# Three halves of expert weights moved from the attention part to behind its last cast and later, and the expert part cut finer

## The chip, the cores and the metric

One core of one Trainium2 chip. The metric is the device time of one execution in microseconds (us), lower is better. Unless said otherwise a time is the median of several unprofiled runs, and positions in time ("at 109 us") count from the start of a profiled run's span. A core's five engines work side by side: TensorE (PE, with its weight loads as PEld), VectorE (DVE), ScalarE (ACT), GpSimd (Pool) and SyncE (SP). Sixteen DMA engines move data; in this kernel SP issues the loads of q, k, v and the attention's stores (queue q1 of the profile), Pool issues expert weights, gathers and scatters (queue q0).

## The reference, cut to what matters

```python
# attention: 4 batches x 8 heads, 768 tokens of 64; 3 heads causal, 5 with a window of 64 and 4 sinks
x = attention(q, k, v)                      # [3072, 512]
do_compute = x @ w_skip > 0                 # tokens that go through an expert
e_idx = argmax(x[do_compute] @ w_gate, 1)   # one of 8 experts each
for e in range(8):
    h = relu(xc[e_idx == e] @ w1[e])        # 512 -> 1024
    y[e_idx == e] = gate * (h @ w2[e])      # 1024 -> 512
out = x;  out[do_compute] += y
```

The weights are 8 x 2 matrices of 512 x 1024 in float32: 33.6 MB to read. "A half" below is one of these 16 matrices (1 MB once cast to 16 bits), "a quarter" half of it.

## The kernel before

Attention runs over 16 pairs of heads. Results go to `out` in DRAM; then each expert's rows are gathered from `out`, worked on, and scattered back. Weights are loaded in a fixed order from a list, wherever the program calls for the next ones, so all of them share one queue in the order of the calls.

```python
todo = [(e, half, qt) for e in range(E) for half in range(2) for qt in range(2)]

def load_weight(quarters=2):
    e, half, q0 = todo[0]
    del todo[:quarters]
    nc.gpsimd.dma_start(out=<tile of e, half>, in_=<weights, float32>)   # cut

# weigh(i, hi): values of pair i (cut)
    if not last:
        ins = nc.gpsimd.tensor_copy(x16s[i], xh[:, :, h2:h2 + 2])
        if i in (0, 5, 10, 11, 12, 13):
            with tc.issue_after(ins.ins):
                load_weight()

# gate_transpose(i) (cut)
    if i == NPR - 2:
        nc.gpsimd.drain()
    if i == NPR - 1:
        nc.gpsimd.tensor_copy(mark, xTg[:, 0, :1])
        load_weight()

# expert part
    gather(0, 4); load_weight(1)
    gather(4, 6); load_weight(1)
    gather(6, 8); load_weight()
    rows(0); first(0); rows(1)
    for e in range(E):
        if e + 2 < E:
            first(e + 1)
            t = 4 * (e + 2)
            if t < NT:
                gather(t, t + 4)
            if todo:
                load_weight(1 if len(todo) == 2 else 2)
            rows(e + 2)
        second(e)            # its two scatters are issued here, by Pool
        # ... (cut)
```

`load_weight` takes two quarters unless told otherwise. `rows` casts and transposes an expert's 256 gathered rows, `first` and `second` are its two products. `nc.gpsimd.drain()` is an instruction at which Pool's queue stands still for a while; how long, and behind what, the traces below show. The values of `v` arrive in two buffers, so pair i + 2 is loaded once pair i is cast by Pool (`cast_v`).

The softmax here doesn't subtract the row's maximum and nothing guards it: scores larger than these inputs give would overflow.

Of the kernel before, what the change touches and what calls it, by code (L numbers as in the profile page):

```python
# [9 lines left out]
FP32 = mybir.dt.float32  # L10
FP16 = mybir.dt.float16
# [4 lines left out]
ACT = mybir.ActivationFunctionType  # L16
# [11 lines left out]
DM = H * D  # L28
E = 8
# [4 lines left out]
P = 128  # L34

DS = DM // P
FS = F // P
CAP = 256
# [3 lines left out]
WR = 4  # L42
# [217 lines left out]
def kernel(  # L260
# [14 lines left out]
    nc = tc.nc  # L275
    C = Consts()
# [77 lines left out]
    wts = {}  # L354
# [19 lines left out]
    def load_weight(quarters=2):  # L374

        e, half, q0 = todo[0]
        q1 = q0 + quarters
        assert q1 <= 2
        del todo[:quarters]
        if half == 0:  # L380
            w = DS * F // 2
            nc.gpsimd.dma_start(
                out=wts[e, 0].rearrange("p s f -> p (s f)")[
                    :, q0 * w:q1 * w], in_=w1r[e][:, q0 * w:q1 * w])
        else:
            nc.gpsimd.dma_start(
                out=wts[e, 1].rearrange("p (t r) d -> p t (r d)", r=WR)[
                    :, q0:q1],
                in_=w2r[e][:, q0:q1])
# [20 lines left out]
    with tc.tile_pool(name="ac", bufs=1) as ac_pool, \  # L410
# [29 lines left out]
        NPR = B * H // 2  # L440
# [62 lines left out]
        def cast_v(i):  # L503
            va, vx = vab[i % 2], vxb[i % 2]
            nc.gpsimd.tensor_copy(va[:, :, :, :D], v32[i])  # L505
            if i:
                nc.scalar.activation(xgs[i], xgs[0], ACT.Copy)  # L507
            for hi, hh in enumerate(heads(i)[1]):
                if not IS_RETR[hh]:
                    nc.gpsimd.tensor_copy(vx[:, hi], va[:, hi, :NQB - 1])  # L510
                    nc.gpsimd.tensor_copy(
                        vx[:N_SINK, hi], va[:N_SINK, hi, 0:1].to_broadcast(
                            [N_SINK, NQB - 1, D + 1]))

        def transpose(i, name):
            tps = tr_psum.tile([P, S], FP16, tag="tps", name="tps")
# [92 lines left out]
        def weigh(i, hi):  # L609
            b, hs = heads(i)  # L610
            b0 = base(i, hi)
            va, vx = vab[i % 2], vxb[i % 2]
            if IS_RETR[hs[hi]]:
                plan = [(qb, RCOL[j, qb], va[:, hi, j])
                        for qb in range(NQB) for j in range(qb + 1)]
            else:
                plan = []
                for qb in range(NQB):
                    plan.append((qb, qb * P, va[:, hi, qb]))
                    if qb:  # L620
                        plan.append((qb, (NQB - 1 + qb) * P,
                                     vx[:, hi, qb - 1]))
            opsa = ov_psum.tile([P, NQB, D + 1], FP32, tag="opsa",
                                name="opsa")
            for n, (qb, c, vb) in enumerate(plan):
                nc.tensor.matmul(  # L626
                    opsa[:, qb, :], ats[i][:, b0 + c:b0 + c + P], vb,
                    start=(n == 0), stop=(n == len(plan) - 1))
            if i % 2 == 0 and hi == 0:
                xhs[i // 2] = x_pool.tile([P, NQB, 4, D], FP32, tag="xh",  # L630
                                          name="xh")
            last = i == NPR - 1
            if hi == 0:
                x16s[i] = gat_pool.tile([P, NQB, 2, D], FP16, tag="gx16",
                                        name="gx16", bufs=2)
            rec = o_pool.tile([P, NQB, 1], FP32, tag="rec", name="rec")
            nc.vector.reciprocal(rec, opsa[:, :, D:D + 1])  # L637
            if last:
                nc.vector.tensor_mul(x16s[i][:, :, hi], opsa[:, :, :D],
                                     rec.to_broadcast([P, NQB, D]))  # L640
            nc.vector.tensor_mul(xhs[i // 2][:, :, 2 * (i % 2) + hi, :],  # L641
                                 opsa[:, :, :D],
                                 rec.to_broadcast([P, NQB, D]))
            if hi == 0:
                return
            xh = xhs[i // 2]
            h2 = 2 * (i % 2)
            if not last:
                ins = nc.gpsimd.tensor_copy(x16s[i], xh[:, :, h2:h2 + 2])  # L649
                if i in (0, 5, 10, 11, 12, 13):  # L650
                    with tc.issue_after(ins.ins):
                        load_weight()
            if i >= NPR - 2:
                nc.sync.dma_start(
                    out=Ov[b][:, :, hs[0] * D:(hs[1] + 1) * D].rearrange(
                        "p n (h d) -> p n h d", h=2),
                    in_=xh[:, :, h2:h2 + 2])
            elif i % 2 == 1:
                hc = (i // 2) % 2
                nc.sync.dma_start(  # L660
                    out=Ov[b][:, :, hc * 4 * D:(hc + 1) * 4 * D],
                    in_=xh.rearrange("p n h d -> p n (h d)"))
# [250 lines left out]
    with tc.tile_pool(name="moe_w", bufs=1) as mw_pool, \  # L913
# [19 lines left out]
        def gather(t0, t1):  # L933
            for t in range(t0, t1):
                ins = nc.gpsimd.indirect_dma_start(  # L935
                    out=xgs[t], out_offset=None, in_=out[:, :],
                    in_offset=bass.IndirectOffsetOnAxis(
                        ap=idx_s[:, t:t + 1], axis=0),
                    bounds_check=N - 1, oob_is_err=False)
                apart(ins)  # L940
                gathers[t] = ins.ins

        xTs, hts = {}, {}

        def rows(e):

            xT = mx_pool.tile([P, DS, CAP], FP16, tag="xT", name="xT")
            x16s = []
            for s2 in range(NSM):
                x16 = mx_pool.tile([P, DM], FP16, tag="x16", name="x16")  # L950
                nc.vector.tensor_copy(
                    x16.rearrange("p (s r) -> p s r", s=DS),
                    xgs[e * NSM + s2].rearrange("p (r s) -> p s r", s=DS))
                x16s.append(x16)
            for s2, x16 in enumerate(x16s):
                xtp = xt_psum.tile([P, DS, P], FP16, tag="xtp", name="xtp")
                for s in range(DS):
                    nc.tensor.matmul(xtp[:, s, :], x16[:, s * P:(s + 1) * P],
                                     C.ident, is_transpose=True,
                                     start=True, stop=True)  # L960
                nc.vector.tensor_copy(xT[:, :, s2 * P:(s2 + 1) * P], xtp)  # L961
            xTs[e] = xT

        def first(e):
            ht = h_pool.tile([P, FS, CAP], FP16, tag="ht", name="ht")
            for f2 in range(FS // 2):
                hps = h_psum.tile([P, 2, CAP], FP32, tag="hps", name="hps")
                for fi in range(2):
                    fs = 2 * f2 + fi
                    for s in range(DS):  # L970
                        nc.tensor.matmul(  # L971
                            hps[:, fi, :],
                            wts[e, 0][:, s].rearrange(
                                "p (t c r) -> p t r c", c=P, r=WR)[
                                    :, fs // WR, fs % WR],
                            xTs[e][:, s, :], start=(s == 0),
                            stop=(s == DS - 1))
                nc.scalar.activation(ht[:, 2 * f2:2 * f2 + 2], hps, ACT.Relu)  # L978
            hts[e] = ht
# [33 lines left out]
        with tc.manual_schedule(engines={mybir.EngineType.Pool,  # L1013
                                         mybir.EngineType.PE,
                                         mybir.EngineType.DVE}):
            gather(0, 4)
            load_weight(1)
            gather(4, 6)
            load_weight(1)
            gather(6, 8)  # L1020
            load_weight()
            rows(0)
            first(0)
            rows(1)
            for e in range(E):
                if e + 2 < E:
                    first(e + 1)
                    t = 4 * (e + 2)
                    if t < NT:
                        gather(t, t + 4)  # L1030
                    if todo:
                        load_weight(1 if len(todo) == 2 else 2)
                    rows(e + 2)
                second(e)
                if e == E - 2:
                    first(e + 1)
                if todo:
                    load_weight(1 if len(todo) < 3 else 2)
                if e == E - 2:


                    nc.gpsimd.drain()
# [39 lines left out]
```

## Time and profile before

| | before |
|---|---|
| time, median of 4 runs (range) | 206.7 us (205.48 to 207.62) |
| the profiled run | 203.35 us, span 201.9 us |
| DMA, share of 16 engines' span | q0 50.3%, q1 44.3% |
| PE busy / DVE / ACT / POOL | 81% / 54% / 56% / 59% |
| attention's last rows ready, first gather, first product | 120.4, 127.1, 133.1 us |
| last weight lands, PE ends, span ends | 190.4, 192.8, 201.9 us |

How to read it: no compute engine is near full over the whole span, but DMA is, at 94.6%. In the expert part PE has hardly a gap either (59.0 us busy of the 60 from 133 us on). The profiled run is faster than each of the four timed ones, so its 201.9 us of span lies at the fast end. Below, three groups of lines from the kernel before stand for what later changes. First, three stretches of the expert part (stretch, length, then busy us of PE, PEld, DVE, ACT and POOL with numbers of instructions, then PE's granted clock, DMA share, GB/s):

```profile
133.00:146.00 13.00, 12.18 (x103) 10.14 (x103) 5.30 (x11) 4.78 (x8) 10.47 (x11) 1.00 1.00 228
146.00:154.00 8.00, 8.00 (x64) 6.10 (x62) 4.04 (x8) 2.55 (x5) 5.29 (x6) 1.00 1.05 232
154.00:190.40 36.40, 36.40 (x268) 26.38 (x267) 14.53 (x26) 11.79 (x20) 17.70 (x20) 1.00 1.01 236
```

DMA is at 1.00 or a little above in all three (a share above 1 is packets that overlap on an engine). PE is busy for 12.18 of 13 us in the first and to the hundredth in the other two. Second, Pool's drain and the load behind the last transpose (start, length, engine, what):

```profile
L682 POOLq DRAIN  x1: 5147/5147/5147, 115.3 to 115.3; - x1
120.54 0.19 POOL L685 COPY mark<-gxT 128x1 f16<-128x1 f16 x1 [4.27 <-DVE gxT L678]
121.01 0.56 POOL L382 DMA_DIRECT2D w<-in_moe_w_dram  x1 [0.28 <-issue]
127.13 1.10 POOL L935 DMA_INDIRECT xg<-out_dram,idx_s  x1 [4.06 <-DVE flagi L910]
```

The drain took 5.1 us here. It ended at 120.4, 0.5 us after the copy (DVE, at 119.9) that Pool had to wait for next. The routing's next small Pool instruction waited for DVE until 122.6 in any case, so the drain held no gather. Third, the expert 6 products on PE:

```profile
174.88 3.66 PE L971 MATMUL hps<-xT,w 128*128 128x256 f16 x32
```

There is no bracket behind it: PE did not wait for the weights.

### The profile page before, as it was taken

How to read it: one execution, taken by the hardware profiler on the slowest of the kernel's cores; microseconds unless marked ns; L12 is line 12 of the kernel's file. 1: busy time of each engine (PE TensorE's matmuls, PEld its weight loads, DVE VectorE, ACT ScalarE, POOL GpSimd, SP SyncE). 2: the span in 40 equal slices, each digit the busy share in tenths (PEclk: the TensorE clock that was granted, in tenths of full speed). 3: DMA queues.
4: the chain of work that ended last, by engine and by line, in shares of the span. 5: the costliest groups of instructions: out<-in, count | busy, mean ns of one | idle time of the engine just before them, and what ended most of it. 6: DMA issues, size and time to landing. Idle time of an engine off the chain costs nothing.

```text
span 201.9 us, 4741 instructions
## 1 busy us (share of the span) xinstructions
PE 163.2 (81%) x1896; PEld 119.3 (59%) x1896; DVE 109.5 (54%) x254; ACT 113.0 (56%) x164; POOL 119.3 (59%) x179
## 2 busy tenths in 40 slices
PE   0487999889888898888982757978999999999920
PEld 0366666676666676666852443378678678665700
DVE  5323666636899668997650678253444534534020
ACT  5998888897688977888891420035143144130400
POOL 7585499687387693788403901687858575133311
PEclk9999999999999999999998795999999999999985
DMA  5999699999899999999999899479999999999501
GB/s 173 295 345 287 169 174 238 316 327 318 236 245 201 301 343 296 342 266 214 215 275 232 204 234 174 103 181 246 232 239 233 239 245 233 235 245 248 165 14 63
DMA packets 47856, 47.12 MB, mean 233 GB/s; under 512 B 28484, under 2 KB 43588, under 8 KB 46802
## 3 DMA queue, kind: packets, MB, share of 16 engines
q0 software_dynamic: 6976, 21.56, 50.3%
q1 hardware_dynamic: 40850, 25.17, 44.3%
q8 instruction: 17, 0.28, 0.6%
q14 instruction: 13, 0.11, 0.2%
HBM read 56.64 MB, written 10.49 MB: 333 GB/s over the span
## 4 chain that ended last, share of the span: by engine, by line
ACT 27%; DMA 26%; PE 23%; issue 8%; DVE 7%; POOL 6%; POOLq 1%; SPq 0%; ACTq 0%; DVEq 0%
ACT at L606 15%; DMA out_dram<-xg,idx_s 14%; DMA vf<-in_v_dram 10%; PE pst L578 5%; ACT xg L507 4%; PE pst L588 4%; PE hps L971 4%; ACT qT L526 4%; ACT gxT L675 3%; PE opsa L626 3%; POOL out_dram L1001 2%; PE pst L595 2%; PE yps L991 2%; POOL xg L935 2%; DMA xg<-out_dram,idx_s 1%
## 5 line engine op out<-in xcount | busy, mean ns | idle before, releaser
L606 ACT ACTIVATE at<-pst 128x1024 f16<-128x1024 f32 (+2 forms) x76 | 61.3, 836 | 17.2 <-PE pst L600 13.3
L978 ACT ACTIVATE ht<-hps 128x512 f16<-128x512 f32 x32 | 19.1, 598 | 49.4 <-PE hps L971 49.4
L588 PE MATMUL pst<-qT,kz 128*128 128x128 f16 (+2 forms) x288 | 35.8, 242 | 2.5 <-ACT qT L526 2.1
L588 PEld LDWEIGHTS <-kz 128*128 128x128 f16 x288 | 24.1, 100 | 21.9 <-issue 12.8
L535 DVE COPY kz<-tps 64x768 f16<-64x768 f16 x28 | 26.6, 950 | 9.7 <-PE tps L518 9.3
L971 PE MATMUL hps<-xT,w 128*128 128x256 f16 x256 | 29.2, 273 | 1.2 <-DVE xT L961 1.2
L971 PEld LDWEIGHTS <-w 128*128 128x128 f16 x256 | 27.9, 113 | 2.8 <-issue 1.5
L578 PE MATMUL pst<-smask,ident 128*128 128x512 f16 (+1 forms) x60 | 22.3, 372 | 8.7 <-ACT at L606 8.7
L991 PE MATMUL yps<-w,ht 128*128 128x512 f16 x128 | 28.8, 379 | 0.0
L1001 POOL DMA_INDIRECT out_dram<-xg,idx_s x16 | 16.4, 1022 | 18.5 <-issue 8.5
L649 POOL CAST gx<-xh 128x768 f16<-128x768 f32 x15 | 12.4, 828 | 19.3 <-DVE xh L641 14.5
L999 DVE SCALAR_TENSOR_TENSOR xg<-yps,gsl,xg 128x512 f32<-128x512 f32 x16 | 12.0, 750 | 20.4 <-PE yps L991 20.3
L626 PE MATMUL opsa<-va,at 128*128 128x65 f16 x372 | 19.8, 196 | 4.0 <-POOL va L505 4.0
L935 POOL DMA_INDIRECT xg<-out_dram,idx_s x16 | 16.8, 1047 | 8.6 <-issue 4.3
L626 PEld LDWEIGHTS <-at 128*128 128x128 f16 x472 | 17.9, 99 | 5.4 <-issue 4.2
L505 POOL CAST va<-vf 128x768 f16<-128x768 f32 x16 | 14.0, 876 | 11.2 <-DMA vf<-in_v_dram 11.1
L637 DVE RECIPROCAL rec<-opsa 128x6 f32<-128x6 f32 x32 | 6.2, 194 | 26.3 <-PE opsa L626 25.9
L991 PEld LDWEIGHTS <-ht 128*128 128x128 f16 x128 | 12.3, 98 | 13.5
L641 DVE TENSOR_TENSOR xh<-opsa,rec 128x384 f32<-128x384 f32 x32 | 17.8, 556 | 1.3
L499 POOL CAST qin<-qf 128x768 f16<-128x768 f32 x16 | 13.1, 818 | 3.3 <-DMA qf<-in_q_dram 3.3
L499 POOL CAST kin<-kf 128x768 f16<-128x768 f32 x16 | 13.1, 822 | 1.0 <-DMA kf<-in_k_dram 0.8
L518 PE MATMUL tps<-ident,qin 128*128 128x128 f16 x96 | 8.7, 231 | 5.9 <-POOL qin L499 5.9
(117 smaller groups left out, 260.7 us busy)
## 6 DMA issues: line engine op xcount, KB each, us to landing
w<-in_moe_w_dram POOLq DMA_DIRECT2D x14, 1024.0 KB, 10.7
qf<-in_q_dram SPq DMA_DIRECT2D x16, 384.0 KB, 6.3
kf<-in_k_dram SPq DMA_DIRECT2D x16, 384.0 KB, 6.0
vf<-in_v_dram SPq DMA_DIRECT2D x32, 192.0 KB, 6.0
out_dram<-xh SPq DMA_DIRECT2D x7, 768.0 KB, 6.8
w<-in_moe_w_dram POOLq DMA_DIRECT2D x4, 512.0 KB, 12.4
out_dram<-xh SPq DMA_DIRECT2D x2, 384.0 KB, 5.2
xg<-out_dram,idx_s POOLq DMA_INDIRECT x16, 7.2
```

The source lines that it names most:

```text
L499: nc.gpsimd.tensor_copy(h16, qk32[name, i].rearrange("p h n d -> p n h d"))
L535: nc.vector.tensor_copy(to, ti[r])
L578: nc.tensor.matmul(pst[:, bank - c0:bank - c0 + mw], C.ident, rmask.unsqueeze(1).to_broadcast([P, mw // P, P]) if retr else smask[:, bank: ...
L588: nc.tensor.matmul(pst[:, cols], kz[:, j * P:(j + 1) * P], qT[i][:, qb * P:(qb + n) * P], start=mw <= 0, stop=mw <= 0 or last)
L606: nc.scalar.activation(ats[i][:, b0:b0 + cn], pst[:, :cn], ACT.Exp, scale=SCALE)
L626: nc.tensor.matmul(opsa[:, qb, :], ats[i][:, b0 + c:b0 + c + P], vb, start=(n == 0), stop=(n == len(plan) - 1))
L641: nc.vector.tensor_mul(xhs[i // 2][:, :, 2 * (i % 2) + hi, :], opsa[:, :, :D], rec.to_broadcast([P, NQB, D]))
L935: ins = nc.gpsimd.indirect_dma_start(out=xgs[t], out_offset=None, in_=out[:, :], in_offset=bass.IndirectOffsetOnAxis(ap=idx_s[:, t:t + 1], ...
L971: nc.tensor.matmul(hps[:, fi, :], wts[e, 0][:, s].rearrange("p (t c r) -> p t r c", c=P, r=WR)[:, fs // WR, fs % WR], xTs[e][:, s, :], sta ...
L978: nc.scalar.activation(ht[:, 2 * f2:2 * f2 + 2], hps, ACT.Relu)
L991: nc.tensor.matmul(ypss[s2], hts[e][:, fs, s2 * P:(s2 + 1) * P], wts[e, 1][:, fs, :], start=(fs == 0), stop=(fs == FS - 1))
L1001: ins = nc.gpsimd.indirect_dma_start(out=out[:, :], out_offset=bass.IndirectOffsetOnAxis(ap=idx_s[:, t:t + 1], axis=0), in_=xgs[t], in_off ...
```

## The change

Its intent, as one reads it from the code: three halves of weights no longer compete with the last loads of v (Pool waited 10.1 us for one of them), and fill instead the hollow in DMA traffic around the first gathers. The expert part is cut finer so that it can start after one gather.

```diff
 # cast_v(i)
+            if i == NPR - 1:
+                load_weight()
+                load_weight()
 # weigh
-                if i in (0, 5, 10, 11, 12, 13):
+                if i in (0, 5, 10):
 # expert part
-            gather(0, 4)
+            gather(0, 2)
+            load_weight(1)
+            gather(2, 4)
             load_weight(1)
             gather(4, 6)
             load_weight(1)
             gather(6, 8)
-            load_weight()
-            rows(0)
-            first(0)
+            load_weight(2 if len(todo) % 2 == 0 else 1)
+            first_by_tile(0)          # 128 rows at a time: 64 matmuls of 128 columns for 32 of 256
             rows(1)
+            second(0)
+            rows(2)
+            first(1)
             for e in range(E):
+                if 0 < e < E - 2:
+                    first(e + 1)
                 if e + 2 < E:
-                    first(e + 1)
                     t = 4 * (e + 2)
                     if t < NT:
                         gather(t, t + 4)
                     if todo:
-                        load_weight(1 if len(todo) == 2 else 2)
+                        load_weight(1 if len(todo) < 3 or len(todo) % 2 else 2)
-                    rows(e + 2)
-                second(e)
+                    if e:
+                        rows(e + 2)
+                if e:
+                    second(e)
 # (cut: row() and first_by_tile() themselves; the last load's parity)
```

More of the change, by code (lines that the diff above doesn't have):

```diff
@@ L943, with row @@
         xTs, hts = {}, {}
+        def row(e, s2):
+            if s2 == 0:
+                xTs[e] = mx_pool.tile([P, DS, CAP], FP16, tag="xT", name="xT")
+            x16 = mx_pool.tile([P, DM], FP16, tag="x16", name="x16")
+            nc.vector.tensor_copy(
+                x16.rearrange("p (s r) -> p s r", s=DS),
+                xgs[e * NSM + s2].rearrange("p (r s) -> p s r", s=DS))
+            xtp = xt_psum.tile([P, DS, P], FP16, tag="xtp", name="xtp")
+            for s in range(DS):
+                nc.tensor.matmul(xtp[:, s, :], x16[:, s * P:(s + 1) * P],
+                                 C.ident, is_transpose=True,
+                                 start=True, stop=True)
+            nc.vector.tensor_copy(xTs[e][:, :, s2 * P:(s2 + 1) * P], xtp)
         def rows(e):
@@ L962, in rows, with first_by_tile @@
             xTs[e] = xT
+        def first_by_tile(e):
+            ht = h_pool.tile([P, FS, CAP], FP16, tag="ht", name="ht")
+            hpss = [h_psum.tile([P, 2, CAP], FP32, tag="hps", name="hps")
+                    for _ in range(FS // 2)]
+            for s2 in range(NSM):
+                cols = slice(s2 * P, (s2 + 1) * P)
+                if s2 == 0:
+                    row(e, 0)
+                for fs in range(FS):
+                    if s2 == 0 and fs == FS - 3:
+                        row(e, 1)
+                    for s in range(DS):
+                        nc.tensor.matmul(
+                            hpss[fs // 2][:, fs % 2, cols],
+                            wts[e, 0][:, s].rearrange(
+                                "p (t c r) -> p t r c", c=P, r=WR)[
+                                    :, fs // WR, fs % WR],
+                            xTs[e][:, s, cols],
+                            start=(s == 0), stop=(s == DS - 1))
+                    if s2 == NSM - 1 and fs % 2:
+                        nc.scalar.activation(ht[:, fs - 1:fs + 1],
+                                             hpss[fs // 2], ACT.Relu)
+            hts[e] = ht
         def first(e):
@@ L1037 @@
                 if todo:
-                    load_weight(1 if len(todo) < 3 else 2)
+                    load_weight(1 if len(todo) < 3 or len(todo) % 2 else 2)
                 if e == E - 2:
```

## The prediction

> **What bounds the kernel now.** I read the page's slices first, then the chain that ended last, the waits, the Pool timeline around the largest wait, the DMA queues in short windows, and PE and DMA stretch by stretch. The slices show the DMA row at 9 nearly everywhere, with one hollow just after the attention part (slices 26 and 27, 126 to 136 us) and one at the end.
>
> ```profile
> DMA  5999699999899999999999899479999999999501
> q0 software_dynamic: 6976, 21.56, 50.3%
> q1 hardware_dynamic: 40850, 25.17, 44.3%
> ```
>
> The two queues together keep the 16 engines at work for 94.6% of 201.9 us, that is 191 us. q0 carries weights, gathers and scatters (issued by Pool), q1 carries q, k, v and the attention stores (issued by SyncE). The waits and the Pool timeline (start, length, engine, line) name the one great stall:
>
> ```profile
> POOL va L505 <- DMA vf<-in_v_dram: 11.1, 2, 10.1
> 98.29 0.56 POOL L382 DMA_DIRECT2D w<-in_moe_w_dram  x1
> 108.94 0.83 POOL L505 CAST va<-vf 128x768 f16<-128x768 f32 x1 [10.09 <-DMA vf<-in_v_dram]
> ```
>
> Pool could have cast v of pair 14 at 98.3 us and did so at 108.9. In the chain this is one piece of 19.65 us. PE used up its other work and stood still for 4.03 us before the values of pair 14 (109.82 us). The DMA engines meanwhile did not rest; by stretch (us, then busy time of PE, PEld, DVE, ACT, POOL, then clock, DMA share, GB/s):
>
> ```profile
> 99.00:109.00 10.00, 6.04 (x92) 4.36 (x90) 4.31 (x17) 7.42 (x10) 0.06 (x1) 1.00 1.02 239
> 109.00:121.00 12.00, 7.83 (x122) 5.80 (x122) 6.87 (x18) 3.41 (x5) 7.00 (x12) 0.82 0.97 228
> 121.00:127.00 6.00, 4.99 (x36) 2.35 (x34) 5.02 (x25) 0.24 (x1) 0.97 (x3) 0.50 0.95 185
> 127.00:133.00 6.00, 4.94 (x27) 2.17 (x26) 2.04 (x4) 0.00 (x0) 4.81 (x5) 1.00 0.39 99
> 133.00:193.00 60.00, 59.02 (x440) 43.50 (x439) 24.75 (x45) 19.12 (x32) 33.46 (x36) 1.00 0.98 226
> ```
>
> The last row matters most. In the expert part PE has no gap, and DMA has none either: both are full at once. The two are matched to within a microsecond. The last quarter of weights is issued at 173.54 us and takes 16.9 us to land, so it lands at 190.4; PE starts the last expert's second product at 189.22 (16 matmuls, 216 ns apart), and its second half, which needs that quarter, at about 190.95. Slack: 0.5 us.
>
> **What a transfer costs, and who goes first.** Packets, MB and share in windows of 2 us: the first line at 92 us, the second at 114, the third pair at 63 us, the fourth at 94 us, the last at 120 us.
>
> ```profile
> q0 software_dynamic: 51, 0.42, 101.0%
> ...
> q0 software_dynamic: 93, 0.38, 97.1%
> ...
> q0 software_dynamic: 95, 0.39, 95.8%
> q1 hardware_dynamic: 94, 0.02, 9.1%
> ...
> q1 hardware_dynamic: 1241, 0.31, 70.4%
> ...
> q1 hardware_dynamic: 1024, 0.51, 84.2%
> ```
>
> Share times 32 engine-us over packets gives the time of one: 0.63 us (8 KB, first product's weights), 0.33 us (4 KB, second's), 18 ns (256 B of v), 26 ns (512 B of the last two stores). A half of an expert's weights (1 MB written) is 128 or 256 packets over 16 engines: 5.1 or 5.3 us. A pair's v, 1536 packets, takes 1.75 us; a 768 KB store about 2.3 us (0.67 MB in 2 us at 99.4%, window at 110 us); the last two stores, 1536 packets, 2.5 us.
>
> The Trainium skill, DMA: Bandwidth & Descriptors, section "Queues, rings and completion order", says each engine goes round-robin between queues with work, packet by packet; the same page, "Issuing engines are not separate DMA queues", that transfers issued from any engine share the same 16. The trace agrees: at 63 us 95 weight packets pass against 94 packets of v. But one weight packet lasts as long as 18 of v, so v gets 9% of the time. This is why v of pair 14, issued at 88.7 behind weights of pair 10 and followed by those of 11 and 12, needed 19.7 us and not the median 6.0.
>
> **The change part by part.**
>
> Removed: the three halves issued behind pairs 11, 12 and 13 (92.9, 98.3, 111.5 us). Only pair 10's half (87.3) then meets v of pair 14. At pair 5 the same meeting cost Pool no wait, so v 14 should land near 99 us and the 10.1 us wait go to 0 to 1 us. PE gains its 4.0 us, plus about 1.2 us lost to the half clock that followed (the stretch 109 to 121 has a clock of 0.82; the 21 value matmuls took 1.26 us there against 0.78 in earlier pairs). The attention and routing chain comes 5.2 us earlier: indices ready at 121.9 and not 127.1.
>
> Moved: two halves behind the cast of v 15. That cast stands behind pair 13's, which needs DVE's result at 104.3, so it starts at about 104.9; with four copies (0.47 us each) Pool issues them at 107.7 and 108.5, and their packets start near 109. The third comes with the old one after the last transpose (121.0 less 5.2, about 115.8). What came there before (the first half for expert 3) goes in quarters behind gathers.
>
> DMA account, 88 to 109 us after: one half 5.1, two v 3.5, two stores 4.6, rest of q and k 1.1: 14.3 of 21 us, so 6.7 us of new idleness, which before had none. The hollow that the change wants to fill is 6 x 0.61 = 3.7 us at 127 to 133, with small gaps 4.2 us.
> From 109 to 190.4 before: 81.4 less 4.2 idle, 77.2 us of work. After, from 109: 77.2 plus two halves 10.4, less what of v and of pair 13's store was still to do at 109, about 4.2: 83.4 us. Without any gap the last weight lands at 109 + 83.4 = 192.4, 2.0 us later than before; less the 0.5 slack, the end moves 1.5 us later, however early PE starts.
>
> Then the stores of pairs 14 and 15, which every gather must await. The skill's same DMA page, "Two DMAs through the same engine are not ordered", says the dependent DMA must be issued after the first one's completion semaphore. They are issued at about 110.0 and 114.2 and need 96 packets per engine. Over weights 1 to 1 they get some 27 turns until q0 empties near 124.8 (three halves of 5.1 from 109, with the part of the stores served); the other 69 packets x 26 ns end near 126.7. The gathers then start at about 127, as before: the 5.2 us are lost again. Before, the store of pair 14 already showed this: issued at 115.29, it landed 6.2 us later, as one half ended, and not a packet of it passed in the window at 116. In that case q0 stands idle from 124.8 till the first quarter behind two gathers flows at about 131, of which stores and gathers fill half: 3 us more.
>
> First expert by tiles: PE can start after one gather, about 1 us earlier; 64 matmuls of 128 columns for 32 of 256 are the same array time (four scores of 128 columns take 0.22 us, 55 ns each, against 109 for 256). Second(0) before first(1) and rows(2) only reorder PE; the first scatters now stand in Pool's queue before gathers 8 to 11, and Pool's next whole halves are issued about 22 us after the gathers start, which may starve q0 for 1 to 2 us. One half more than before is outstanding at the gathers.
>
> Sum: 1.5 (new idleness against hollow filled), plus 0 to 3 (gathers held by stores), plus 0 to 2 (dry queue): 1.5 to 6.5, middle 3.3 us on 201.9: +1.6%. On the median of 207.48 this is 210.8; I take 210.5.
>
> **Rivals.** First, PE sets the end: it starts 6 us earlier, has no gap before or after, and the end comes 6 us earlier: 201.3. For it: 59 of 60 us busy in the last part. Against it: DMA at 0.98 there with 0.5 us of slack. The share of weights still to come when PE starts grows by one half.
> Second, stores are not starved (turns of several packets for q1, as at 88 us, where 70 packets of q passed in a microsecond beside 14 of weights): gathers at 122 to 123, weights flow without a gap: +1.5 us, 209.
> Third, stores starve wholly: gathers at 128 to 129, PE idle in between and, as the skill says (TensorE: Matmul & The Clock Gate, "Part 1: The HAM clock gate"), at half clock after idleness; here 0.50 at 121 to 127 follows the idle stretch before it. First products at half clock cost 2 to 3 us more of PE, which may hide behind the weights: 213 to 215.
> Fourth, unprofiled runs (205.5 to 207.6, against 203.35 for the profiled one) may have a longer v stall, which the change would save: 203 to 206.
>
> **Range and chances.** The account of DMA work is the firmest part and allows hardly any gain, so faster by over 2% gets 0.11, mainly for the fourth rival and for what I can't see of a change made by someone who tuned this kernel. The middle lies just under the 2% line: within 2% 0.48, slower by over 2% 0.41. Range 205.0 to 215.0.
>
> **What would show each step.** Right: Pool's wait for v gone; a DMA hollow at 100 to 109 us; pair 14's and 15's stores taking 10 us or more to land; first gather near 127 us though the indices are ready near 122; PE with gaps in the expert part that weights end; the last weight landing after 192. Wrong: first gather at 122 and no PE gap after it (first rival), or the last weight landing before 189, which would mean that I miscounted the idle DMA time. Then the kernel is faster.

## The result, and the profile after

| | before | after |
|---|---|---|
| time, median (range) | 206.7 (205.48 to 207.62) | 213.58 (213.25 to 213.85) |
| span of the profiled run | 201.9 | 212.2 |
| first gather, first product | 127.1, 133.1 | 128.0, 134.7 |
| last weight issued, landed | 173.5, 190.4 | 183.9, 200.8 |
| from there to the end | 11.5 | 11.4 |

The ratio is 1.0336, 95% interval 1.0268 to 1.0404: slower. Ratios here and below are the mean time of one kernel's fast runs over that of the other's fast runs of the same rounds, so they are not quite the ratio of the medians quoted. A run counts as slow when it is over 1.5% above the fastest of its kernel.

The chain of the changed kernel's page broke off at its last instruction (it shows only entries of 0%), so I read the waits, the stretches and the timelines. The stretches first, columns as above:

```profile
99.00:109.00 10.00, 9.25 (x156) 6.84 (x154) 6.92 (x22) 8.81 (x13) 5.80 (x10) 1.00 0.34 105
109.00:121.00 12.00, 5.95 (x84) 3.65 (x81) 8.23 (x28) 2.23 (x4) 1.64 (x3) 0.76 0.98 182
121.00:127.00 6.00, 0.91 (x9) 0.60 (x9) 1.17 (x6) 0.00 (x0) 1.31 (x4) 0.50 0.66 145
127.00:133.00 6.00, 5.50 (x22) 2.07 (x19) 0.73 (x6) 0.00 (x0) 4.07 (x5) 0.85 1.00 195
133.00:146.00 13.00, 10.28 (x100) 7.86 (x100) 6.56 (x13) 2.17 (x4) 8.86 (x10) 0.87 1.03 248
146.00:154.00 8.00, 7.93 (x78) 7.81 (x79) 2.21 (x6) 4.69 (x8) 6.47 (x8) 1.00 0.56 118
154.00:200.80 46.80, 42.88 (x294) 29.48 (x293) 16.80 (x30) 12.03 (x21) 20.84 (x23) 0.96 1.01 225
```

The stall that the change was after is gone: at 99 to 109 PE is busy for 9.25 us where it was 6.04. But DMA fell to 0.34 there. The old hollow at 127 to 133 is filled (1.00, it was 0.39). Two more have opened, at 121 to 127 (0.66) and at 146 to 154 (0.56). Idle DMA time, length times what the share lacks of 1: 6.6, 2.0 and 3.5 us, against 3.7 in the old hollow.

The whole account from 88 us, where the two kernels begin to differ, to the landing of the last weight, first for the kernel before and then for the changed one (queue, packets, MB, share):

```profile
q0 software_dynamic: 5192, 19.01, 85.4%
q1 hardware_dynamic: 6562, 3.55, 11.6%
```

```profile
q0 software_dynamic: 5439, 19.09, 79.3%
q1 hardware_dynamic: 6474, 3.43, 10.4%
```

With 0.5% of instruction fetches in each, that is 97.5% of 102.4 us, so 99.8 us of work and 2.6 idle, against 90.2% of 112.8 us, so 101.7 us of work and 11.1 idle. The difference, 8.5 us of idleness and 1.9 of work, is 10.4 us, and the span grew by 10.3. "Work" here is the time of packets: the bytes were no more than before (22.66 MB in all against 22.71). And this is bookkeeping: idle time and packet time must add up to the landing of the last weight, so the sum alone does not show what the end waited for. That is for PE's waits and the experiments.

Pool's timeline between attention and gathers, changed kernel:

```profile
98.55 0.83 POOL L505 CAST va<-vf 128x768 f16<-128x768 f32 x1 [0.23 <-DMA vf<-in_v_dram]
105.13 0.84 POOL L505 CAST va<-vf 128x768 f16<-128x768 f32 x1
108.55 0.70 POOL L386 DMA_DIRECT2D w<-in_moe_w_dram  x1
109.24 0.56 POOL L382 DMA_DIRECT2D w<-in_moe_w_dram  x1
123.78 0.19 POOL L689 COPY mark<-gxT 128x1 f16<-128x1 f16 x1 [13.15 <-issue]
124.24 0.70 POOL L386 DMA_DIRECT2D w<-in_moe_w_dram  x1 [0.27 <-issue]
125.24 0.20 POOL L765 TENSOR_TENSOR val<-gate,val 128x6 f16<-128x6 f32 x1
128.01 1.11 POOL L939 DMA_INDIRECT xg<-out_dram,idx_s  x1 [2.57 <-DVE flagi L914]
```

The casts of the last two v are on time. Then Pool does nothing from 110.6 to 123.8; the waits put that down to "issue", which means that no semaphore shows. Pool's queue has the reason, and the waits tell who stood behind it:

```profile
L686 POOLq DRAIN  x1: 13951/13951/13951, 109.7 to 109.7; - x1
PE sums L771 <- DVE Rall L823: 7.0, 1, 7.0
DVE Rall L823 <- POOL val L765: 6.6, 1, 6.6
```

The drain lasts 13.95 us and ends at 123.7. The first of the two halves, issued at 108.55, landed 9.0 us later; the second, issued at 109.24, landed 14.1 us later, at 123.3, 0.4 us before the drain ended. The drain of before likewise ended at 120.4, 0.4 us after the one half in flight had landed (111.5 + 8.5 = 120.0). In both kernels it thus ends just behind the weights that Pool has under way. The routing needs two small Pool instructions (`val`) that stand behind it, DVE waits 6.6 us for them, PE 7.0. At the same time the last two stores, which every gather has to await, landed at 109.7 + 14.4 = 124.1 and 113.8 + 11.5 = 125.3. So two waits ended at about the same time, and the drain's ended last. In e1 below, where the last half had landed 2.6 us before the drain began, it lasted 2.0 us.

The same store of 384 KB, the last one, first in the changed kernel and then in e5 below, where no weights stand before it (KB, us from issue to landing):

```profile
out_dram<-xh SPq DMA_DIRECT2D x1, 384.0 KB, 11.5
out_dram<-xh SPq DMA_DIRECT2D x1, 384.0 KB, 2.8
```

Short windows show how the time went. From the first store's issue at 109.7 until 113.8 not one packet of a store passed; then weights and stores took turns one to one (48 and 47 packets in the microsecond from 114); when the weights ran out at about 121.3, most of the stores was still to do. In e5 the first packet came 0.9 us after the issue. Why the stores got no turn for 4.1 us is open.

What PE waited for in the expert part (its waits from 133 us on), and where the longest stood:

```profile
PE hps L1016 <- DMA w<-in_moe_w_dram: 3.9, 2, 3.4
183.65 5.21 PE L1016 MATMUL hps<-xT,w 128*128 128x256 f16 x32 [3.43 <-DMA w<-in_moe_w_dram]
```

That is expert 6's first product: at 183.65 in place of 174.88, after 3.43 us of waiting, and then at a lowered clock (5.21 us for work that took 3.66). From it to the end PE has no gap.

These waits are not the whole delay of PE. The first product of expert 3, in the kernel before and in the changed one:

```profile
152.71 3.66 PE L971 MATMUL hps<-xT,w 128*128 128x256 f16 x32
157.19 3.66 PE L1016 MATMUL hps<-xT,w 128*128 128x256 f16 x32
```

So PE was 4.5 us behind before it had waited for any weights: it began 1.6 us later, worked on the first expert at a lowered clock (0.87 at 133 to 146), and waited 1.4 us for the rows of expert 1. The waits for weights (3.9 us) and the lowered clock after the longest (1.55) make up most of the rest, of 10.3 us at the end of PE's work (203.2 against 192.8).

### The profile page after: what moved, and what is told of

Same layout as the page of the kernel before. It is cut to its first block, busy times and chain, and to the rows that moved or that the text cites. A ratio compares the mean times of both kernels' runs of the same rounds, so it can differ in the third digit from the quotient of the medians.

```text
span 212.2 us, 4805 instructions
## 1 busy us (share of the span) xinstructions
PE 164.8 (78%) x1928; PEld 119.9 (57%) x1928; DVE 109.8 (52%) x254; ACT 112.8 (53%) x164; POOL 121.0 (57%) x180
## 2 busy tenths in 40 slices
DMA packets 48000, 47.12 MB, mean 222 GB/s; under 512 B 28500, under 2 KB 43604, under 8 KB 47074
## 3 DMA queue, kind: packets, MB, share of 16 engines
HBM read 56.64 MB, written 10.49 MB: 316 GB/s over the span
## 5 line engine op out<-in xcount | busy, mean ns | idle before, releaser
L592 PE MATMUL pst<-qT,kz 128*128 128x128 f16 (+2 forms) x288 | 35.2, 239 | 2.6 <-ACT qT L530 2.2
L1016 PE MATMUL hps<-xT,w 128*128 128x256 f16 x224 | 27.0, 282 | 3.9 <-DMA w<-in_moe_w_dram 3.9
L582 PE MATMUL pst<-smask,ident 128*128 128x512 f16 (+1 forms) x60 | 21.7, 361 | 9.3 <-ACT at L610 9.3
L1016 PEld LDWEIGHTS <-w 128*128 128x128 f16 x224 | 24.8, 115 | 6.6 <-DMA w<-in_moe_w_dram 4.9
L1036 PEld LDWEIGHTS <-ht 128*128 128x128 f16 x128 | 12.3, 98 | 13.5
L630 PE MATMUL opsa<-va,at 128*128 128x65 f16 x372 | 19.2, 193 | 0.0
L630 PEld LDWEIGHTS <-at 128*128 128x128 f16 x472 | 17.4, 97 | 1.2
L980 DVE COPY xT<-xtp 128x512 f16<-128x512 f16 x14 | 5.4, 420 | 20.7 <-PE xtp L977 20.6
```

The lines of the kernel that those rows point to most:

```text
L582: nc.tensor.matmul(pst[:, bank - c0:bank - c0 + mw], C.ident, rmask.unsqueeze(1).to_broadcast([P, mw // P, P]) if retr else smask[:, bank: ...
L592: nc.tensor.matmul(pst[:, cols], kz[:, j * P:(j + 1) * P], qT[i][:, qb * P:(qb + n) * P], start=mw <= 0, stop=mw <= 0 or last)
L630: nc.tensor.matmul(opsa[:, qb, :], ats[i][:, b0 + c:b0 + c + P], vb, start=(n == 0), stop=(n == len(plan) - 1))
L1016: nc.tensor.matmul(hps[:, fi, :], wts[e, 0][:, s].rearrange("p (t c r) -> p t r c", c=P, r=WR)[:, fs // WR, fs % WR], xTs[e][:, s, :], sta ...
L1036: nc.tensor.matmul(ypss[s2], hts[e][:, fs, s2 * P:(s2 + 1) * P], wts[e, 1][:, fs, :], start=(fs == 0), stop=(fs == FS - 1))
```

## The experiments

Twelve runs; each has runs of the kernel before on the same chip (e1 to e10 on one chip, e11 and k1 to k3 on another). The changed kernel was not timed again in any of them, so a difference to its 213.58 us is one between calls. Theory A is the account above, in short: DMA work sets the end, and the change makes DMA idle. B blames the new order of the expert part, C Pool's drain alone, D the time at which PE's expert part starts. Three kernels (e6, e7, e11) compute a wrong result on purpose; the comparison with the reference passed them all the same, so its tolerance does not see one expert's half.

### e1: weights back, the rest of the change kept

```diff
 # changed kernel
-            if i == NPR - 1:
-                load_weight()
-                load_weight()
-                if i in (0, 5, 10):
+                if i in (0, 5, 10, 11, 12, 13):
```

> The changed kernel with the three halves of weights put back behind pairs 11 to 13; the quarters behind gathers, the first expert by tiles and the third expert's rows stay. Theory A (DMA account: the moved weights leave the DMA engines idle at 99 to 109 us and hold the gathers): DMA is full again at 99 to 109, the v stall of some 10 us is back, first gather near 127, last weight lands at 188 to 192 (a quarter earlier into the hollow against a dry queue at the first scatters), time 203 to 209, ratio to before 0.985 to 1.01. Theory B (the new order of the expert part costs the time): ratio 1.02 or more, last weight after 195.

Measured: median 207.59 us, ratio 0.9997 (0.989 to 1.0103). Two of its five runs were slow, the profiled one among them, so I take from it only that Pool again waited 9.9 us for v. The ratio is what A expected, and B falls: the quarters behind gathers, the first expert by tiles and the new order together cost nothing that this interval of 1% shows with the weights in their old place. They gain nothing either.

### e2: only the weights moved

```diff
 # kernel before
+            if i == NPR - 1:          # end of cast_v
+                load_weight()
+                load_weight()
-                if i in (0, 5, 10, 11, 12, 13):
+                if i in (0, 5, 10):
-                        load_weight(1 if len(todo) == 2 else 2)
+                        load_weight(1 if len(todo) < 3 else 2)
```

> The kernel before with only the three halves moved (two behind the cast of the last v, the third with the one after the last transpose); expert part in the old order. Theory A: DMA idle for 6 to 7 us at 99 to 109, Pool's drain takes about 14 us, first gather at 127 to 129, last weight at 195 to 200, ratio 1.015 to 1.035, the rest to the changed kernel being the dry queue at the first scatters (about 3 us). Theory B: ratio under 1.01.

Measured: 211.56 us, ratio 1.0238 (1.0127 to 1.035), span 209.5. Drain 14.6 us, first gather at 128.7. Two stretches of it:

```profile
99.00:109.00 10.00, 9.25 (x156) 6.84 (x154) 6.29 (x21) 8.81 (x13) 6.19 (x10) 1.00 0.45 136
146.00:154.00 8.00, 8.00 (x68) 6.11 (x67) 3.38 (x7) 2.72 (x6) 5.05 (x6) 1.00 1.07 235
```

The move alone makes the first hollow (0.45, 5.5 us) and most of the loss, but not the one at 146 to 154. The remainder to the changed kernel, 2.7 us of span, is about what was expected for that one. How the loss reaches the end is less plain than theory A has it: PE's first product came at 136.2, 3.1 us later than before, and took 5.32 us for 3.65, while its waits for weights add up to 1.3 us. So e2 shows that the move costs the time, but most of it came here through PE's late and slow start.

### e3: the changed kernel without the drain

```diff
-            if i == NPR - 2:
-                nc.gpsimd.drain()
```

> The changed kernel without Pool's drain after the transpose of the last but one pair. Theory A as predicted (the last two stores, behind weights, hold the gathers): first gather still at 126 to 128 us, as the third half is now issued near 116 and starves the stores longer; time within 2% of the changed kernel, 209 to 214. Theory C (Pool's drain, which waits for the two halves of weights, is what holds routing and gathers): indices and first gather at 122 to 124, time 4 us or more under the changed kernel.

Measured: 216.28 us, ratio 1.0488 (1.0403 to 1.0574): slower than with the drain, and above what A had expected. C falls. The indices were ready by 121.9 us, yet the first gather came at 131.6, at the end of 13.5 us in which Pool stood idle:

```profile
115.04 0.70 POOL L386 DMA_DIRECT2D w<-in_moe_w_dram  x1
131.57 1.11 POOL L937 DMA_INDIRECT xg<-out_dram,idx_s  x1 [13.54 <-issue]
```

Without the drain the third half was issued at 115.0. The last store had been issued 0.7 us before, but nearly all packets of both stores were still to come (29 had passed), so they shared with this half too: both stores landed at 129.4 and 130.5 (19.1 us after 110.3, 16.1 after 114.4). The queues at 123 to 125 us in this run:

```profile
q0 software_dynamic: 95, 0.39, 95.6%
q1 hardware_dynamic: 96, 0.05, 12.0%
```

One packet of a store for one of weights, 95 to 96, and so 12% of the DMA time for the stores that everything waited for. I had expected the first gather at 126 to 128; I had let q0 empty at 124.8, and it did near 128.

### e4: without the drain, the third half later

```diff
 # e3, and:
                 nc.gpsimd.tensor_copy(mark, xTg[:, 0, :1])
-                load_weight()
 # behind the third and fourth pair of gathers: load_weight(2) each
```

> As the one without the drain, and the third half is not issued after the last transpose but in whole halves behind the sixth and eighth gather, so that nothing starves the stores after 121 us. Both A and C: first gather at 122 to 124. Theory A (DMA work sets the end): last weight lands no earlier than 195, time 208 to 214, though PE starts 4 to 5 us sooner. Theory D (the start of PE's expert part sets the end): time under 207.

Measured: 214.47 us, ratio 1.0405 (1.0307 to 1.0503). First gather at 128.0, not 122 to 124: a miss for all theories. The last store was issued at 115.0 and landed 12.0 us later, at 127.0, though only the two halves behind the cast of the last v stood before it. So the two halves alone, with no drain and no third half, hold the gathers as long as in the changed kernel. But PE did not start early, so D was not tested.

### e5: all three behind the gathers

```diff
 # changed kernel, no drain, neither the two loads behind the cast nor the one behind the last transpose;
 # gather(0, 2), (2, 4), (4, 6), (6, 8) with load_weight(2) behind each
```

> The changed kernel without the drain, all three moved halves issued only behind the gathers (a half behind each two), so that nothing stands before the last two stores. Stores land near 118 to 120, first gather at 122 to 123 (5 us before the kernel before), PE's first expert product near 129. Theory A (DMA work sets the end): DMA idle 99 to 122 costs more than ever, last weight lands after 203, ratio 1.04 or more. Theory D (an earlier start of the expert part brings an earlier end): ratio under 1.02.

Measured: 217.13 us, ratio 1.0479 (1.034 to 1.0618). This is the test of D. The first gather is at 123.6, held by the indices alone, and PE's first product at 128.6, 4.5 us before that of the kernel before. Two DMA stretches, PE's longest waits and one of its places:

```profile
109.00:121.00 12.00, 8.06 (x116) 5.46 (x114) 9.40 (x30) 3.65 (x6) 2.80 (x6) 0.72 0.26 79
121.00:127.00 6.00, 5.39 (x30) 2.31 (x28) 1.91 (x12) 0.00 (x0) 2.92 (x3) 1.00 0.09 25
PE hps L1009 <- DMA w<-in_moe_w_dram: 9.6, 3, 5.5
179.09 5.25 PE L1009 MATMUL hps<-xT,w 128*128 128x256 f16 x32 [5.51 <-DMA w<-in_moe_w_dram]
```

DMA did little for 18 us (14.3 of them idle), and PE paid for it later: 9.6 us of waits for weights. It started 4.5 us earlier and the kernel was 4.8% slower, all four runs above all seven of the kernel before. D falls in the form that an earlier start brings an earlier end. But the lead was gone before the weights ran out: PE waited 4.3 us for the rows of expert 1, and its first product of expert 3 came at 156.2, 3.5 us later than before. So e5 does not tell what a late start costs.

### e6, e7 and e11: a half of weights taken away

```diff
 # e6 (changed kernel) and e7 (kernel before; there also the parity of one load, cut): the last half, expert 7's second matrix
-            for qt in range(2)]
+            for qt in range(2)][:-2]
+                if (e, half) == (E - 1, 1):
+                    wts[e, half] = wts[e - 1, half]
 # e11 (changed kernel): expert 3's second matrix in the same way
```

> The changed kernel with the last expert's second half of weights not loaded (that of the expert before is used in its place; wrong result on purpose). It takes 5.2 us of DMA work away and no PE work. Theory A: 4 to 6 us less than the changed kernel, ratio to before 1.005 to 1.02. Theory D: within 1 us of the changed kernel, ratio 1.03 or more.

> The same removal in the kernel before (wrong result on purpose). As PE had no gap in the expert part there, with 0.5 us of slack for the last quarter: both theories expect it within 1% of before, ratio 0.99 to 1.005. A ratio under 0.985 would say that DMA alone set the end of before too.

> The changed kernel with the second half of expert 3 not loaded (expert 2's in its place; wrong result on purpose): the same 5.2 us of DMA work as the last half, but ahead of the first half of expert 6, for which PE waited last. Theory A, refined (DMA work up to the half of the longest wait sets the end; what comes after it was ready in time): 3.5 to 5.5 us under the changed kernel, ratio to before 1.005 to 1.02, PE's wait for weights of 3.4 us gone. Theory D: within 1.5 us of the changed kernel.

e6 measured 211.88 us, ratio 1.026 (1.0127 to 1.0393): 1.7 us under the changed kernel's median, not the 4 to 6 that A had said. Its trace still has PE's wait of 3.4 us for expert 6's first half. The last half lies behind that one in the queue, and was in time. So it is not the last landing that sets the end of PE's work, but the DMA work up to the half of the longest wait; that is why e11 was made. e7 measured 204.2 us, ratio 0.985 (0.9696 to 1.0005): more than the 1% that I had allowed, with an interval that reaches 1.

What both won is seen in their traces, and it is no shorter wait of PE. In e6 PE ended at 203.15, in the changed kernel at 203.16. In e7 PE had no wait for weights, as in the kernel before, and took the same 59.7 us from its first product to its last. What shrank is the tail from PE's end to the end of the span: 6.8 us in both, against 9.0 and 9.1 in the kernels they were made from. The second drain of Pool, near the end of the loop's cut part (at expert 6), does it. Here are that drain and the first of the last two scatters in the changed kernel, then the same scatter in e6:

```profile
L1094 POOLq DRAIN  x1: 7949/7949/7949, 197.0 to 197.0; - x1
205.85 0.98 POOL L1046 DMA_INDIRECT out_dram<-xg,idx_s  x1 [6.91 <-issue]
203.35 0.98 POOL L1048 DMA_INDIRECT out_dram<-xg,idx_s  x1 [6.37 <-DVE xg L1046]
```

The drain ends at 204.9, and the scatter behind it starts 2.5 us later than in e6, where the drain ends at 200.6 and only DVE's result is awaited, which was ready at the same time in both. In the kernel before it likewise ends at 194.6, after DVE's first result (192.8). Without the last half the drain was shorter (4.8 us for 7.9, and 4.6 for 6.7 in e7). No run here was made without this drain.

e11 measured 209.44 us (208.37 to 210.83): 4.1 us under the changed kernel, as expected, and PE's work from 154 to 190 us is without a gap:

```profile
154.00:190.00 36.00, 36.00 (x262) 25.19 (x260) 16.30 (x29) 10.88 (x19) 17.47 (x19) 1.00 1.03 223
```

PE's last product thus ended 4.6 us earlier than in the changed kernel, though its first had come 1.4 us later. But without any wait for weights until the last product (0.4 us) PE was still 5.2 us behind the kernel before (expert 3's first product at 157.86), and e11 was slower than it. So about 4 us are what the late weights cost; the rest, some 3 us, PE's late and slow start would have cost even with weights in time.

Its ratio, 1.0282 (1.0183 to 1.0382), is above the expected 1.005 to 1.02. The kernel before had runs from 202.48 to 210.24 us without a break, and six of eleven counted as slow because the fastest was so fast, so the ratio is to its five best; to the median of all (205.99) it would be 1.017. I read the effect from the two kernels' own times and the wait that vanished, and hold the size for roughly known. They were run at other times. The same goes for e6 and e10.

### e10: gathers before the first scatter

```diff
 # changed kernel
             rows(1)
+            gather(8, 12)
+            load_weight(2)
             second(0)
 # and neither of them again in the loop for e = 0
```

> The changed kernel with gathers 8 to 11 and the half behind them issued before the first expert's second product, so that its scatters no longer stand before them in Pool's queue. Theory A: the DMA share at 146 to 154 us rises from 0.56 to over 0.9 and the time falls by 2 to 4 us, ratio 1.015 to 1.03. Rival: the dry stretch costs nothing because a later wait takes its place; within 1 us of the changed kernel.

Measured: 211.22 us, ratio 1.0218 (1.0082 to 1.0353), 2.4 us under the changed kernel's median, span 209.4 against 212.2.

```profile
146.00:154.00 8.00, 7.31 (x70) 7.14 (x71) 2.91 (x6) 3.94 (x7) 6.24 (x8) 1.00 1.01 219
```

The hollow is full (1.01 for 0.56). It came from the order in Pool's queue: the first expert's two scatters waited for its second product, and gathers 8 to 11 and the next whole halves stood behind them. Filling 3.5 us of it gave 2.4 to 2.8 us, and PE's longest wait for weights fell from 3.4 to 0.5 us. PE was then 5.5 us behind at expert 3 (158.21), so its own late start seems by then the nearer limit.

### k1, k2 and k3: three tries at a better version

```diff
 # kernel before; k1:
-                if i in (0, 5, 10, 11, 12, 13):
+                if i in (0, 5, 10, 11, 13):
+            if i == NPR - 1:          # end of cast_v
+                load_weight()
                 nc.gpsimd.tensor_copy(mark, xTg[:, 0, :1])
-                load_weight()
+                load_weight(1)
 # gathers (0, 2), (2, 4), (4, 6), (6, 8), with 1, 1, 1 and 2 quarters behind them
 # k2: k1 without the drain
 # k3: k2 without the load behind the last transpose; 1, 1, 2 and 2 quarters behind the gathers
```

> A version meant to be better: the kernel before with only pair 12's half taken from its place (pairs 11 and 13 keep theirs), one half behind the cast of the last v, a quarter after the last transpose, and quarters behind each two gathers. Weights then never stand before two v loads in a row, and DMA stays full. Pool's wait for v under 3 us, first gather at 122 to 126, DMA share at 99 to 109 over 0.85; time 200 to 205, ratio 0.97 to 0.99. If the drain holds Pool until the half behind the cast has landed, the gathers come at 125 or later and the gain is under 1%.

> As the other without Pool's drain: first gather 1 to 3 us sooner than with it if the drain held it, else the same; ratio 0.965 to 0.99.

> As the second of the two meant to be better (one half moved, no drain), with the quarter after the last transpose put behind the gathers, so that no weights stand before the last store after 117 us. First gather at 121.5 to 123.5, PE's first expert product at 127 to 129. If the end of before is set by PE's start (its expert part had no gap there), the time is 198 to 202, ratio 0.97 to 0.985; if DMA work sets it as in the changed kernel, PE gets gaps that weights end and the ratio is 0.99 to 1.01.

Measured: k1 205.94 us, ratio 1.0108 (1.0015 to 1.0201); k2 205.02, ratio 1.007 (0.9993 to 1.0147); k3 205.3, ratio 1.0073 (0.9998 to 1.0148). None beats the kernel before, and all three miss the ratios expected of a gain (k1's under 1% in case of the drain, and k3's 0.99 to 1.01 for DMA, are what came). As for e11, only the best five of eleven runs of before counted as fast; against all its runs (medians 205.99 and 206.0) the three are level with it (three of k1's six runs counted as slow too). The mechanics were in part as meant: v no longer holds Pool (0.3 us in k2 and k3, no such wait in k1), DMA is full at 99 to 109, and k1's first gather is at 125.8, with an 11.8 us drain before it. Without the drain the gathers were still late: k2's first came at 127.1 (1 to 3 us sooner than k1's had been expected), k3's at 125.5 and its first product at 131.0 (121.5 to 123.5 and 127 to 129 expected). k3's stretches:

```profile
99.00:109.00 10.00, 9.25 (x144) 6.88 (x144) 6.16 (x24) 8.06 (x13) 3.96 (x7) 1.00 1.02 270
121.00:127.00 6.00, 5.54 (x27) 2.33 (x25) 3.12 (x15) 0.00 (x0) 1.18 (x2) 0.73 0.36 92
127.00:133.00 6.00, 4.47 (x35) 3.11 (x34) 1.96 (x4) 0.66 (x2) 5.09 (x6) 1.00 0.73 140
```

DMA is as full before 121 us as in the kernel before, but idle for 5.5 us from there to 133 (3.8 and 1.6), against 4.0 there. PE started 2.1 us before the kernel before did, had lost all but 0.15 us of that at expert 3 to waits for gathered rows, and waits for weights again in two places (0.4 and 0.8 us). In k1's profiled run, which has no wait for weights, the first product is 1.4 us earlier and the span 0.9 us shorter than before (201.0), but its timed runs show no gain. With PE and DMA as closely matched as here, an earlier start of one alone hardly moves the end.

## Why the prediction was right or wrong

The direction and the range held (205 to 215, measured 213.58); the middle, 210.5, was 3.1 us low. It was set on 207.48 us, one of the four times of the kernel before; their median is 206.7, so the loss was 6.9 us where 3.3 were said. By its steps:

- **The v stall goes, and this gains nothing at the end.** Right. Pool's wait fell from 10.1 to 0.2 us, the cast of the last v came at 105.1 (104.9 said), the two halves at 108.6 and 109.2 (107.7 and 108.5 said).
- **New idleness of 6.7 us at 88 to 109, against a filled hollow.** Right: 6.6 us at 99 to 109, none before, and the old hollow at 127 to 133 is at 1.00. e2, with the move alone, has a like hollow (5.5 us) and most of the loss.
- **DMA work, not the start of PE, sets the end.** Right for the last 4 us of the changed kernel's loss: e11 took DMA work away and won them back, e10 won 2.4, and e5 started PE 4.5 us earlier and was 4.8% slower. The form in which I put it, by the landing of the last weight, was too simple: that came 10.4 us later and the end 10.3 later, but e6 showed that PE did not wait for it, and e11 that what stood before expert 6's half mattered. And PE's own delay is missing from the sum: 4.5 us at expert 3 without a wait for weights. Only the third rival had a slow start of PE (2 to 3 us).
- **The last two stores, behind weights one to one, hold the gathers until about 127.** The time was right (stores landed at 125.3, first gather 128.0), in part by luck; the cause was only half. I had not seen Pool's drain, which kept Pool for 13.95 us and with it the two instructions that routing needs; in the changed kernel it ended later than the stores. I had also let the third half be issued at 115.8, and behind the drain it came at 124.2, so that two halves and not three stood before the stores. That was made up by something else that I missed: the stores got no turn at all for 4.1 us, and some 15 turns per engine in place of 27. My own line had said so, the window at 116 us without a packet of the store, which does not fit turns of one to one. (The 27 do not follow from the packet counts either: halves of 256, 128 and 256 packets are 40 per engine.) e3 and e4 show that the wait for the stores is real and enough by itself: without the drain the first gather is at 131.6 and 128.0.
- **A dry queue at the first scatters, 0 to 2 us.** The mechanism was right, the term too small: 3.5 us idle at 146 to 154; filling it, e10 was 2.4 to 2.8 us faster.
- **The sum.** I had 1.5 us for the new idleness against the filled hollow, after 0.5 us of slack, 0 to 3 for a late first gather and 0 to 2 for the dry queue, at most 6.5. Measured as idle DMA time it was 6.6 - 3.7 = 2.9 us, then 2.0 (at 121 to 127) and 3.5 (at 146 to 154), 8.4 in all, and 1.9 us more of packet time, which the sum did not have (the bytes were the same): 10.3, as the profiled spans differ. So in this bookkeeping the mis-sized terms are the hollows (2.9 for 1.5), the dry queue (3.5 for at most 2) and the missing one. The timed medians differ by 6.9 us only, because the profiled run of before was at the fast end of its runs.
- **First rival (PE sets the end).** Fell as it was put, with an end 6 us earlier: PE did not start earlier (134.7 for 133.1), and weights came last. That PE is nearly as late a limit, e11 shows. **Second** (stores not starved): fell, stores behind weights took 11.5 to 19.1 us to land and, once they had turns, passed one packet for one of weights. **Third** (stores starve wholly, 213 to 215 us): its time and its first gather (128 to 129) are what came, and so is PE's clock of 0.50 at 121 to 127, but the stores starved wholly only for their first 4 us and then got their turns; what it lacked was the drain. **Fourth** (usual runs of before have more to gain): the usual runs of before are slower than the profiled one, but the change was slower than all of them.

What stays open: how the changed kernel's loss divides between late weights and PE's late, slow start (e11 puts the first at about 4 us); what the second drain costs by itself; whether DMA limits the usual, unprofiled runs of the kernel before (e7's interval reaches 1, and its trace shows the gain behind the second drain); and why its runs spread over 4%.

## What to carry to other kernels

Where DMA is full, count its idle time before and after a move of loads: a stall that is removed elsewhere is worth nothing if the engines that set the end are given a hole. Large packets and small ones that take turns one to one share the time in the ratio of their lengths (here about 0.32 us for a weight packet and 0.04 for one of a store, worked out from e3's window: 12% for the stores), so a small transfer that others wait for (a store before a gather) should be issued before large ones, not after. And look at what stands behind a drain or a blocked instruction in the same queue, since it waits too, whatever it needs: here the routing behind the first drain (6.6 us of DVE's time) and the last scatters behind the second (2.5 us).

## What the Trainium skill lacked or had wrong

- DMA: Bandwidth & Descriptors, "Queues, rings and completion order": it says that an engine drains a whole packet, typically 9 to 17 descriptors, before it goes on to the next queue. The records of these runs show, while both queues are steadily at work, turns of one to one (95 of weights to 96 of a store at 123 to 125 us in e3, 95 to 94 in the kernel before), and the page does not draw the consequence: the queue with 512-byte packets got 12% of the time and a 384 KB store took up to 19.1 us to land. Nor does a page give a delay before the first turn: 4.1 us for the first of the last two stores behind weights (109.7 to 113.8), 0.9 us in e5 without them.
- No page that I found says that a drain on Pool outlasts the DMAs that Pool has under way: 5.1 us with one 1 MB load in flight, 13.95 us with two, each ending within 0.5 us of the landing of the last of them (120.0 and 123.3); 2.0 us in e1 with none.
- DMA: Bandwidth & Descriptors, "Bandwidth", and the fit in "Anatomy of one DMA": nothing there prices a load that casts from 4 to 2 bytes. A half of 1 MB written took 5.1 or 5.3 us of all 16 engines here (128 packets of 0.63 us or 256 of 0.33, as the prediction works out), and HBM read 56.64 MB where the DMA records count 47.12 MB.
